# Another order of steps behind the first batch's attention in a fused attention and phase-mixing kernel

## The chip, the cores and the metric

The kernel runs on one core of a Trainium2 chip. The metric is the device time of one execution in microseconds (us); lower is better. The times below are medians over several runs. Five engines work side by side, each with its own queue in program order: TensorE (PE, matmuls and transposes into PSUM), VectorE (DVE), ScalarE (ACT), GpSimd (POOL) and SyncE (SP, which here only issues DMAs). POOL issues DMAs too.

## The reference

Two parts run one after the other, for 4 batches of 768 tokens.

```python
# 1. attention, 8 heads of 64; heads 0, 2 and 6 are causal, the others see
#    the first 4 keys and the last 64
scores = where(mask, scale * q @ k.T, -1e9)
a = exp(scores - max); a = a / sum(a)
x = a @ v                                    # heads side by side: [4, 768, 512]
# 2. phase mixing
theta = x @ w_theta                          # 512 x 512
zr, zi = x * cos(theta), x * sin(theta)
y = w_tok_r @ zr + w_tok_i @ zi              # 768 x 768, over the tokens
u = x + y
out = u + maximum(u @ w_ch, 0)               # 512 x 512
```

Inputs and the output are fp32; the kernel computes in bf16 with fp32 sums.

## The kernel before

Everything is kept in SBUF, and tokens are worked on in 6 blocks of 128. PSUM is one tile of 8 banks (`banks`), and every step that writes PSUM is told its bank or, for two banks, the first of them. Nothing is scheduled by a planner: the string `ORDER` (lines 54 to 105) is the program, a list of 812 steps. A step's name, its arguments and, at the end, its bank or its engine (D for DVE, A for ACT, P for POOL) are joined by dots. Each engine's queue holds its own steps in the order of the list, and a step waits by semaphores for what it reads, and for the readers of what it overwrites (a bank, a buffer). So a step that waits holds up all later steps of its own engine, and a bank named again makes PE wait for the reader of its last content.

The steps, with b the batch:

- `lq`, `lt`, `lw` (lines 228 to 253): POOL issues the load of one pair of heads of q or k, of a block of `w_tok`, of a weight. `lv` (234): SP issues the load of a block of v. `cv`, `bv`, `sv` copy v to bf16 (`vt`), to the block before (`vo`) and its sink rows, on the named engine.
- `tq.b.q.n.bank`, `eq`: PE turns a pair n of q or k in 12 transposes (L263), a copy brings it to `qT` or `kT` (DVE L269, ACT L267). For batch 3 the turn goes by DMA instead: `qi` joins a pair (`xi`), `qx` issues the DMA on SP, `ex` copies the result. `ko` copies keys for the streaming heads.
- `s.b.m.bank`, `e`, `m`: scores of unit m (17 units to a batch, PE L319), exp on ACT (L349), mask on DVE (L359 to L371).
- `av.b.i.bank`, `n`: a @ v of block i (PE L406), and its normalisation on DVE (L411, L413), which writes `x`.
- `xp`, `xe` turn a block of x on PE (batch 0); `xg.b.g` turns a pair of blocks by DMA from SP (the other batches).
- `wt`, `we`: a block of `w_tok` turned on PE (L442) and copied to `wtokT`.
- `th.b.g.bank` (PE L454, 8 matmuls), `tc`, `ts` (ACT L457, L460, cosine and sine into `ct` and `st`, two buffers each), `z.b.g.r/i.y` (L465): theta of two blocks, its cosine and sine, and the four products with x, called phases here, on DVE or POOL. `at` has ACT load the table of sine or exp.
- `mx.b.t.p.bank` (PE L473, 4 matmuls): output block t gets the input blocks 2p and 2p+1; three such steps fill a bank. `u` (DVE L485) adds x. `ud` turns u by DMA from SP into `uT`. `ch` (PE L489, 4 matmuls) is u @ w_ch, `o` (DVE L492) finishes it and `st` (SP) stores it; for the last block `up`, `ue`, `ca`, `oa`, `sa` do the same by PE and in halves.
- `pw.m.n.bank` (PE L512): n matmuls of ones whose result is never read.

In batch b's attention PE also does batch b-1's mixing: their steps alternate in the list. Around each theta stage (`th` of a batch) the chain is PE, ACT, DVE or POOL, then PE again. When the phases of one group are made, the third group's sine and cosine write into the buffers that the first group's phases read.

DVE's and POOL's phases are one line of the same helper:

```python
(nc.vector if eng == "D" else nc.gpsimd).tensor_tensor(z[b % 2][:, i], x[b % 2][:, i], t[:, y], ALU.mult)
```

Of the kernel before, what the change touches and what calls it, by code (L numbers as in the profile page):

```python
# [70 lines left out]
mx.0.2.1.2 s.1.4.6 m.1.15 lv.1.0 e.1.4.6 s.1.5.3 m.1.7 m.1.6 s.1.0.4 lq.2.k.2 e.1.0.4 u.0.2.2 mx.0.0.1.0 e.1.5.3 pw.0.0.6 m.1.9 mx.0.0.2.0 lq.2.q.3
wt.3.0.6 we.3.0.6.D s.1.11.2 e.1.11.2 s.1.3.4 e.1.3.4 m.1.1 lq.2.k.1 m.1.5 mx.0.0.0.0 mx.0.3.1.7 m.1.0 tq.2.k.3.2 u.0.0.0 pw.1.0.5 s.1.10.3 cv.1.1.P
bv.1.1.D m.1.12 m.1.4 m.1.3 s.1.16.0 e.1.16.0 cv.1.0.D bv.1.0.D e.1.10.3 wt.5.0.6 we.5.0.6.D lv.1.2 mx.0.3.2.7 lv.1.4 lq.2.k.0 mx.0.3.0.7 u.0.3.7
wt.5.1.0 eq.2.k.3.2.A bv.1.3.A av.1.0.5 s.1.14.2 lw.c sv.1.P n.1.0.5 e.1.14.2 we.5.1.0.D tq.2.q.3.4 eq.2.q.3.4.A tq.2.k.2.7 eq.2.k.2.7.D m.1.13 lt.4.1
# [8 lines left out]
e.2.11.6 m.2.8 e.2.5.0 mx.1.2.1.2 s.2.0.0 u.1.3.3 e.2.6.4 s.2.3.6 s.2.9.3 lq.3.q.3 qi.3.q.3.D m.2.5 qx.3.q.3 m.2.15 m.2.4 e.2.3.6 mx.1.2.2.2 m.2.6
m.2.12 mx.1.5.0.5 lq.3.k.1 st.0.0 u.1.2.2 lq.3.k.3 qi.3.k.3.D ud.1.2 mx.1.5.1.5 e.2.0.0 s.2.10.0 m.2.3 lq.3.q.2 e.2.9.3 s.2.13.6 ud.1.3 cv.2.1.P
ex.3.k.2.D e.2.13.6 m.2.0 s.2.14.3 qx.3.k.3 m.2.9 lq.3.q.1 lq.3.q.0 cv.2.3.A bv.2.3.P mx.1.5.2.5 u.1.5.5 ud.1.5 qi.3.k.1.D e.2.10.0 bv.2.1.A
mx.1.0.2.2 mx.1.0.0.2 e.2.14.3 av.2.0.0 n.2.0.0 av.2.1.5 n.2.1.5 mx.1.0.1.2 u.1.0.2 xg.2.0 m.2.13 cv.2.5.P ex.3.q.3.A bv.2.2.D av.2.2.3 n.2.2.3
cv.2.4.P bv.2.4.P st.0.2 qx.3.k.1 mx.1.1.2.0 ch.0.4.1 o.0.4.1 av.2.4.6 qi.3.q.1.A n.2.4.6 mx.1.1.0.0 ex.3.k.3.D ko.3.3.A av.2.3.1 n.2.3.1 av.2.5.6
n.2.5.6 xg.2.1 st.0.4 mx.1.1.1.0 u.1.1.0 st.0.5 s.3.8.1 e.3.8.1 xg.2.2 s.3.16.3 ch.1.3.5 th.2.0.6 ex.3.k.1.P ko.3.1.D qi.3.q.2.P ch.1.2.1 qx.3.q.1
e.3.16.3 m.3.16 tc.2.0.6 th.2.1.2 o.1.3.5 z.2.0.r.0.D z.2.0.r.1.D ts.2.0.6 z.2.0.i.0.D mx.1.4.2.4 mx.1.4.1.4 ch.1.5.0 qx.3.q.2 ex.3.q.1.D tc.2.1.2
qi.3.q.0.A th.2.2.6 mx.1.4.0.4 o.1.5.0 ts.2.1.2 ex.3.q.2.A ud.1.1 ch.1.1.3 z.2.0.i.1.P ud.1.0 o.1.2.1 z.2.1.r.1.D z.2.1.i.1.D u.1.4.4 o.1.1.3 ch.1.0.5  # L90
st.1.3 ko.3.2.D lv.3.0 z.2.1.i.0.D m.3.8 lv.3.4 tc.2.2.6 qx.3.q.0 ts.2.2.6 z.2.2.i.0.D o.1.0.5 s.3.13.0 e.3.13.0 lq.3.k.0 z.2.2.r.1.D z.2.2.r.0.D
ud.1.4 s.3.5.4 e.3.5.4 z.2.1.r.0.P s.3.3.2 qi.3.k.0.D mx.2.2.0.7 e.3.3.2 mx.2.1.0.6 mx.2.1.1.6 s.3.14.4 s.3.15.0 s.3.7.2 mx.2.2.1.7 cv.3.0.D
z.2.2.i.1.P qx.3.k.0 mx.2.1.2.6 st.1.5 e.3.7.2 ex.3.q.0.D m.3.3 mx.2.2.2.7 e.3.15.0 e.3.14.4 u.2.1.6 mx.2.5.2.2 lv.3.1 m.3.7 s.3.6.0 e.3.6.0 bv.3.0.D
sv.3.D s.3.9.5 e.3.9.5 s.3.4.3 u.2.2.7 lv.3.3 ud.2.2 e.3.4.3 lv.3.2 ex.3.k.0.P mx.2.5.0.2 mx.2.5.1.2 u.2.5.2 ud.2.5 ch.1.4.7 s.3.2.5 e.3.2.5 s.3.11.2
cv.3.4.P o.1.4.7 st.1.4 cv.3.1.D e.3.11.2 s.3.0.0 m.3.4 m.3.9 bv.3.1.D st.1.1 mx.2.3.1.4 mx.2.4.2.5 st.1.2 m.3.6 s.3.1.2 s.3.10.6 lv.3.5 e.3.0.0 m.3.2
s.3.12.0 e.3.1.2 mx.2.4.1.5 m.3.0 cv.3.3.A ud.2.1 m.3.15 mx.2.4.0.5 m.3.1 av.3.0.2 u.2.4.5 mx.2.3.2.4 bv.3.4.P m.3.13 st.1.0 m.3.5 n.3.0.2 cv.3.5.P
e.3.10.6 e.3.12.0 av.3.1.6 bv.3.3.A mx.2.3.0.4 n.3.1.6 cv.3.2.A m.3.12 ch.2.5.5 o.2.5.5 mx.2.0.2.3 av.3.2.6 xg.3.0 bv.3.2.D mx.2.0.0.3 n.3.2.6 u.2.3.4
av.3.3.1 av.3.5.6 n.3.3.1 av.3.4.4 n.3.5.6 n.3.4.4 ch.2.2.0 o.2.2.0 mx.2.0.1.3 at.1.S th.3.0.6 ts.3.0.6 u.2.0.3 z.3.0.i.0.D st.2.5 ch.2.1.1 o.2.1.1
# [503 lines left out]
```

## Time and profile before

| | |
|---|---|
| median of 3 runs | 178.44 us (178.34 to 180.28) |
| the profiled execution | 179.92 us, span 177.9 us |
| PE busy | 165.6 us, 93% of the span |
| DVE busy | 146.6 us, 82% |
| ACT busy | 117.2 us, 66% |
| POOL busy | 75.8 us, 43% |
| DMA, read and written | 180 GB/s over the span |

The span runs from the first to the last instruction of the profiled execution; its own time is 2.0 us longer. Busy time is the union of an engine's instructions. Matmuls are pipelined and their ends are modelled, so that neighbours overlap. "idle before" is the time in which an engine had nothing running ahead of an instruction, and behind the arrow stands what released it. L473 is line 473.

### The profile page before, as it was taken

To read this page: it belongs to the slowest core of one execution; us is meant where nothing else is said; L and a number is where in the kernel's file an instruction comes from. 1 tells how busy PE (TensorE), PEld (TensorE's weight loads), DVE (VectorE), ACT (ScalarE), POOL (GpSimd) and SP (SyncE) were. 2 spreads that over 40 slices of the span, in tenths; PEclk is the share of its full clock that TensorE was granted. 3 is DMA by queue.
4 is the path that set the end of the run, shared out by engine and by line. 5 is a ranking of instruction groups with operands and counts; after the bars stand their busy time and mean duration, and the time that the engine had idled before them with its cause. 6 is when DMAs were issued, how large, how long until landed. Compare 5 with 4: busy or idle time off the path is not lost.

```text
span 177.9 us, 4285 instructions
## 1 busy us (share of the span) xinstructions
PE 165.6 (93%) x1715; PEld 91.2 (51%) x1715; DVE 146.6 (82%) x286; ACT 117.2 (66%) x141; POOL 75.8 (43%) x105
## 2 busy tenths in 40 slices
...
PEclk9999999999999999999999999999999999999998
...
GB/s 172 211 172 238 201 205 145 169 220 227 206 192 177 101 151 128 218 128 149 229 237 166 192 50 281 161 197 44 179 153 292 119 133 166 89 4 59 119 263 178
DMA packets 68483, 29.90 MB, mean 168 GB/s; under 512 B 54512, under 2 KB 65520, under 8 KB 68464
## 3 DMA queue, kind: packets, MB, share of 16 engines
...
HBM read 25.69 MB, written 6.29 MB: 180 GB/s over the span
## 4 chain that ended last, share of the span: by engine, by line
PE 70%; DVE 18%; issue 7%; ACT 3%; DVEq 0%
PE banks L473 31%; PE banks L489 9%; PE banks L406 8%; PE banks L319 7%; PE banks L454 5%; PE banks L263 3%; PE banks L512 3%; DVE early L465 3%; PE banks L442 2%; DVE qT L269 2%; ACT ct L457 2%; DVE vo L269 1%; DVE zr L465 1%; DVE kT L269 1%; DVE ot L492 1%
## 5 line engine op out<-in xcount | busy, mean ns | idle before, releaser
L349 ACT ACTIVATE P<-banks 128x1024 bf16<-128x1024 f32 (+2 forms) x64 | 56.8, 946 | 13.1 <-PE banks L319 12.8
L473 PE MATMUL banks<-zr,wtokTr 128*128 128x512 bf16 x72 | 27.4, 380 | 0.0
L473 PE MATMUL banks<-early,wtokTr 128*128 128x512 bf16 x72 | 27.4, 380 | 0.0
L473 PE MATMUL banks<-early,wtokTi 128*128 128x512 bf16 x72 | 27.3, 379 | 0.0
L473 PE MATMUL banks<-zi,wtokTi 128*128 128x512 bf16 x72 | 27.3, 379 | 0.0
L489 PE MATMUL banks<-w_ch_sb,uT 128*128 128x512 bf16 x92 | 23.1, 379 | 1.2 <-DMA uT<-u 0.7
L473 PEld LDWEIGHTS <-wtokTr 128*128 128x128 bf16 x144 | 14.0, 98 | 16.1 <-issue 1.5
L319 PE MATMUL banks<-qT,kT 64*128 64x128 bf16 (+3 forms) x240 | 19.6, 247 | 2.8 <-ACT ct L457 1.6
L473 PEld LDWEIGHTS <-wtokTi 128*128 128x128 bf16 x144 | 14.1, 98 | 13.7
L269 POOL CAST vt<-st_v 128x512 bf16<-128x512 f32 x14 | 9.2, 663 | 27.3 <-DMA st_v<-in_v_dram 27.1
L371 DVE TENSOR_TENSOR P<-P,m_stream 128x1024 bf16<-128x1024 bf16 (+3 forms) x36 | 20.4, 581 | 0.4 <-ACT P L349 0.3
L460 ACT ACTIVATE st<-banks 128x1024 f32<-128x1024 f32 x12 | 12.3, 1027 | 10.9 <-PE banks L454 8.3
L406 PEld LDWEIGHTS <-P 128*128 128x128 bf16 x472 | 16.4, 97 | 3.7 <-DVE P L371 1.2
L406 PE MATMUL banks<-vt,P 128*128 128x65 bf16 x372 | 16.9, 193 | 1.0 <-DVE P L371 1.0
L492 DVE SCALAR_TENSOR_TENSOR ot<-banks,u 128x512 f32<-128x512 f32 x23 | 15.7, 691 | 2.4 <-PE banks L489 2.3
L319 PEld LDWEIGHTS <-kT 64*128 64x128 bf16 x240 | 11.0, 94 | 10.3 <-issue 7.5
L457 ACT ACTIVATE ct<-banks,half_pi 128x1024 f32<-128x1024 f32 x12 | 13.3, 1118 | 2.6 <-PE banks L454 2.3
L489 PEld LDWEIGHTS <-uT 128*128 128x128 bf16 x92 | 8.6, 98 | 11.6 <-DMA uT<-u 1.2
L269 POOL COPY vo<-vt 64x384 bf16<-64x384 bf16 (+1 forms) x9 | 9.5, 1060 | 11.0 <-DVE vt L269 6.8
L485 DVE TENSOR_TENSOR u<-early,banks 128x512 bf16<-128x512 bf16 x12 | 8.3, 689 | 6.7 <-PE banks L473 6.7
L512 PE MATMUL banks<-plain 128*128 128x384 bf16 x43 | 10.7, 378 | 2.8 <-DVE plain L191 2.2
L465 DVE TENSOR_TENSOR early<-early,ct 128x512 bf16<-128x512 bf16 x10 | 10.7, 1085 | 2.5 <-ACT ct L457 2.5
...
## 6 DMA issues: line engine op xcount, KB each, us to landing
...
```

Of the source, the lines that this page charges most:

```text
L269: (nc.vector if eng == "D" else nc.gpsimd).tensor_copy(o, i)
L319: nc.tensor.matmul(*mms[g], start=True, stop=True, skip_group_check=True)
L349: nc.scalar.activation(o, two(bank)[:, :, :o.shape[2]], AF.Exp, scale=scale)
L371: nc.vector.tensor_tensor(o, o, mk, ALU.mult)
L406: nc.tensor.matmul(o, l, r, start=(m == 0), stop=True, skip_group_check=True)
L457: nc.scalar.activation(ct[slot("ct", (b, g), TRIG_BUFS)], two(bank), AF.Sin, bias=half_pi)
L460: nc.scalar.activation(st[slot("st", (b, g), TRIG_BUFS)], two(bank), AF.Sin)
L465: (nc.vector if eng == "D" else nc.gpsimd).tensor_tensor(z[b % 2][:, i], x[b % 2][:, i], t[:, y], ALU.mult)
L473: nc.tensor.matmul(one(bank), wtokT[n][:, s, t * 128:(t + 1) * 128], z[b % 2][:, s], start=(done == 1 and s == 2 * p and n == 0), stop=(do ...
L489: nc.tensor.matmul(one(bank), uT[ti(b, t)][:, kk], w_ch_sb[:, kk], start=(kk == 0), stop=(kk == KD - 1))
L492: nc.vector.scalar_tensor_tensor(ot[oi(b, t)], one(bank), 0.0, u[ui(b, t)], ALU.max, ALU.add)
L512: nc.tensor.matmul(one(bank)[:, :384], plain[:, :128], plain, start=True, stop=True, skip_group_check=True)
```

## The change

Only `ORDER` changes, from line 62 on: behind the first batch's first two blocks of attention, up to the end. The list has the same 812 steps, but for the engine and bank at their ends and for the count of some plain matmuls, in another order.

- **Phases.** Ten go from DVE to POOL: z.0.0.i.1, z.0.1.r.0, z.0.1.i.0, z.1.2.r.0, z.2.0.r.0, z.2.0.r.1, z.2.0.i.0, z.3.0.i.0, z.3.1.i.0, z.3.2.r.1. Five go from POOL to DVE: z.1.0.r.1, z.2.0.i.1, z.2.2.i.1, z.3.0.i.1, z.3.2.i.1.
- **Copies, batch 1 and 2's keys.** To ACT: cv.1.1, cv.1.2 (from POOL), we.5.1, eq.2.k.1, ko.2.2 (from DVE). To POOL: bv.1.1 (from DVE), bv.1.2, bv.1.3 (from ACT). To DVE: cv.1.5 (from ACT), qi.3.k.2 (from POOL).
- **Copies, batch 2 and 3.** To ACT: qi.3.k.3, ex.3.k.3, ex.3.q.1, ko.3.2, bv.3.0 (from DVE), cv.2.4, bv.2.3, bv.2.4, cv.3.4, bv.3.4 (from POOL), ue.3.5 (from DVE). To POOL: cv.2.2, bv.2.2, qi.3.k.1, ko.3.1, cv.3.1, bv.3.1 (from DVE), bv.2.1, ko.3.3, qi.3.q.0, cv.3.2, bv.3.3 (from ACT). To DVE: cv.2.3, qi.3.q.1 (from ACT).
- **Steps of DVE, POOL, ACT and SP**: 216 instead of 233, 103 instead of 92, 136 instead of 130, and 91 as before.
- **Plain matmuls.** pw.9 has 2 instead of 1, and pw.0, pw.1 and pw.17 have 1 instead of 0.
- **Banks** of many steps, among them th.1.0 (2 instead of 5), th.1.1 (6 instead of 2), mx.3.3 (0 instead of 3) and up.3.5 (2 instead of 7).
- **Order.** PE: before, tq.1.q.1 stood ahead of s.1.8 and tq.1.k.0 behind it; now the other way round. th.1.0 has mx.0.4.1 ahead of it. SP: ud.1.0 stands directly ahead of xg.2.1; before, it stood seven issues behind xg.2.1. POOL: lq.2.q.0 and lq.2.q.1 stand ahead of all of batch 1's phases, bv.1.1 ahead of sv.1, and seven phases of batch 0 ahead of lt.5.1 and most of batch 2's loads. DVE: sv.3 stands behind u.2.1, u.2.2 and u.2.5; o.2.4 behind all the phases of batch 3's first two groups.

The diff at the first, second and last theta stage (the lines of one place do not match one to one):

```diff
-wt.2.0.3 xe.0.4.7.D th.0.2.5 tc.0.1.0 tq.1.q.3.4 ts.0.1.0 lt.0.1 tq.1.q.1.0 wt.2.1.2 pw.9.1.1 z.0.0.r.0.D hw.1.5 lt.0.0 tc.0.2.5 ko.1.1.D z.0.0.i.1.D
-we.2.0.3.D ts.0.2.5 z.0.2.r.0.P eq.1.q.3.4.D s.1.8.3 e.1.8.3 we.2.1.2.D eq.1.q.1.0.D tq.1.k.0.1 mx.0.2.0.2 z.0.2.i.1.P z.0.2.i.0.P wt.1.0.7
-eq.1.k.0.1.D s.1.1.0 e.1.1.0 we.1.0.7.D lt.5.0 lt.4.0 tq.1.q.2.5 eq.1.q.2.5.A lq.2.k.3 wt.3.1.6 we.3.1.6.D lt.5.1 mx.0.1.0.3 at.6.E z.0.2.r.1.D
-s.1.13.0 s.1.9.6 z.0.1.i.0.D e.1.13.0 s.1.12.4 e.1.12.4 mx.0.1.2.3 z.0.1.r.1.D e.1.9.6 z.0.1.i.1.D mx.0.2.2.2 wt.0.1.4 z.0.1.r.0.D lq.2.q.2 we.0.1.4.D
+z.0.0.i.0.P th.0.1.0 wt.2.0.3 xe.0.4.7.D tc.0.1.0 th.0.2.5 ts.0.1.0 lt.0.0 z.0.0.r.0.D z.0.0.i.1.P tc.0.2.5 hw.1.5 we.2.0.3.D tq.1.q.3.4 wt.2.1.2
+eq.1.q.3.4.D we.2.1.2.D pw.9.2.7 tq.1.k.0.1 s.1.8.3 tq.1.q.1.0 eq.1.k.0.1.D eq.1.q.1.0.D ts.0.2.5 lt.5.0 e.1.8.3 tq.1.q.2.7 z.0.2.r.0.P eq.1.q.2.7.A
+wt.1.0.6 wt.3.1.5 mx.0.2.0.2 s.1.1.0 e.1.1.0 z.0.2.i.0.P we.1.0.6.D z.0.2.i.1.P z.0.1.r.0.P we.3.1.5.D lq.2.k.3 mx.0.1.0.3 s.1.12.4 z.0.2.r.1.D
+z.0.1.r.1.D z.0.1.i.0.P lt.5.1 lq.2.q.2 z.0.1.i.1.D lq.2.q.3 e.1.12.4 s.1.9.6 s.1.13.0 e.1.13.0 e.1.9.6 mx.0.1.2.3 mx.0.2.2.2 wt.0.1.4 we.0.1.4.D
...
-n.1.5.6 wt.4.1.3 we.4.1.3.A av.1.4.1 cv.2.0.P ch.0.1.4 n.1.4.1 ko.2.2.D th.1.0.5 at.2.S lq.2.q.1 ko.2.1.D tc.1.0.5 xg.1.1 qi.3.k.2.P mx.0.4.0.0
-o.0.1.4 lq.2.q.0 ts.1.0.5 z.1.0.r.0.D z.1.0.i.1.D z.1.0.i.0.D z.1.0.r.1.P th.1.1.2 xg.1.2 th.1.2.4 tc.1.1.2 z.1.1.r.0.D mx.0.4.2.0 z.1.1.r.1.P
-ts.1.1.2 z.1.1.i.1.P ts.1.2.4 tc.1.2.4 ud.0.0 mx.0.4.1.0 u.0.4.0 ch.0.0.3 o.0.0.3 ud.0.2 tq.2.q.0.2 ud.0.3 at.5.E sv.2.P eq.2.q.0.2.D tq.2.q.1.7
+n.1.5.6 ts.1.0.2 qi.3.k.2.D o.0.1.4 mx.0.4.0.0 xg.1.2 th.1.1.6 z.1.0.r.1.D z.1.0.r.0.D z.1.0.i.1.D z.1.0.i.0.D ts.1.1.6 tc.1.1.6 z.1.1.r.0.D th.1.2.4
+mx.0.4.2.0 u.0.4.0 ts.1.2.4 tc.1.2.4 lq.2.q.1 ud.0.0 ch.0.0.6 o.0.0.6 ud.0.3 tq.2.q.0.2 eq.2.q.0.2.D z.1.1.i.0.P lv.2.3 z.1.1.r.1.P z.1.1.i.1.P
+s.2.16.0 sv.2.P s.2.8.4 tq.2.q.1.7 eq.2.q.1.7.D z.1.2.r.0.P ud.0.2 ch.0.3.3 o.0.3.3 ch.0.2.2 o.0.2.2 e.2.16.0 lv.2.2 ud.0.5 st.0.1 s.2.2.0 e.2.8.4
...
-xg.3.1 th.3.1.2 tc.3.0.6 z.3.0.r.0.D z.3.0.r.1.D xg.3.2 th.3.2.5 ts.3.1.2 tc.3.1.2 z.3.1.r.1.D z.3.1.i.0.D z.3.1.i.1.D z.3.0.i.1.P z.3.1.r.0.D ud.2.4
-ch.2.4.1 st.2.2 mx.3.4.0.0 tc.3.2.5 ud.2.3 ch.2.3.4 ts.3.2.5 mx.3.2.0.2 mx.3.3.1.3 mx.3.0.1.6 mx.3.1.1.5 o.2.3.4 z.3.2.i.1.P z.3.2.i.0.D mx.3.4.1.0
+ch.2.1.6 o.2.2.2 z.3.0.i.0.P z.3.0.i.1.D o.2.1.6 th.3.1.2 ts.3.1.2 z.3.0.r.0.D z.3.0.r.1.D ch.2.4.0 xg.3.2 th.3.2.4 z.3.1.i.0.P ud.2.0 ud.2.3 st.2.5
+st.1.4 at.1.S tc.3.1.2 z.3.1.i.1.D z.3.1.r.0.D z.3.1.r.1.D ch.2.3.3 mx.3.2.0.1 mx.3.4.0.6 o.2.4.0 o.2.3.3 st.2.3 tc.3.2.4 mx.3.3.0.0 ts.3.2.4
```

## Rows read from the trace of the kernel before

**Rows 1.** Page: engines' busy time, then the granted clock in 40 slices.

```profile
PE 165.6 (93%) x1715; PEld 91.2 (51%) x1715; DVE 146.6 (82%) x286; ACT 117.2 (66%) x141; POOL 75.8 (43%) x105
PEclk9999999999999999999999999999999999999998
```

**Rows 2.** Timeline of PE at its waits: start, length (us), what [idle before <-releaser].

```profile
37.55 0.29 PE L319 MATMUL banks<-qT,kT 64*128 64x128 bf16 x4 [0.36 <-DVE qT L269]
...
77.85 0.29 PE L319 MATMUL banks<-qT,kT 64*128 64x128 bf16 x4 [1.59 <-ACT ct L457]
78.49 0.23 PE L319 MATMUL banks<-qT,kO 64*128 64x128 bf16 x2 [0.24 <-DVE u L485]
79.09 1.24 PE L489 MATMUL banks<-w_ch_sb,uT 128*128 128x512 bf16 x5 [0.26 <-DVE ot L492]
...
116.25 1.04 PE L489 MATMUL banks<-w_ch_sb,uT 128*128 128x512 bf16 x4 [0.68 <-DMA uT<-u]
118.19 0.37 PE L319 MATMUL banks<-qT,kT 64*128 64x512 bf16 x2 [0.33 <-DVE ot L492]
...
128.66 1.02 PE L489 MATMUL banks<-w_ch_sb,uT 128*128 128x512 bf16 x4 [0.31 <-DVE u L485]
```

**Rows 3.** Busy time (x instructions) by stretch: PE, PEld, DVE, ACT, POOL.

```profile
145.00:174.00 29.00, 28.94 (x141) 13.41 (x139) 17.54 (x28) 8.95 (x10) 3.22 (x2) 1.00 0.43 121
```

**Rows 4.** Timeline of PE, a spare matmul; the same in the chain of waits.

```profile
24.51 0.33 PE L512 MATMUL banks<-plain 128*128 128x384 bf16 x1
...
24.67 0.16 PE banks L512
```

**Rows 5.** Timeline of ACT, 64 to 80 us.

```profile
68.59 1.11 ACT L457 ACTIVATE ct<-banks,half_pi 128x1024 f32<-128x1024 f32 x1 [1.03 <-PE banks L454]
75.77 1.02 ACT L460 ACTIVATE st<-banks 128x1024 f32<-128x1024 f32 x1 [2.56 <-DVE early L465]
```

**Rows 6.** Timeline of DVE, 70 to 80 us.

```profile
69.74 2.75 DVE L465 TENSOR_TENSOR early<-early,ct 128x512 bf16<-128x512 bf16 x1 [1.68 <-ACT ct L457]
72.41 3.24 DVE L465 TENSOR_TENSOR early<-early,st 128x512 bf16<-128x512 bf16 x2
75.58 2.27 DVE L465 TENSOR_TENSOR early<-early,ct 128x512 bf16<-128x512 bf16 x1
```

**Rows 7.** Timeline of POOL, 69.5 to 79 us.

```profile
70.02 0.72 POOL L231 DMA_DIRECT2D qb<-in_q_dram  x1
70.76 1.17 POOL L465 TENSOR_TENSOR early<-early,ct 128x512 bf16<-128x512 bf16 x1
75.05 2.24 POOL L269 COPY vo<-vt 4x1920 bf16<-4x1920 bf16 x1
```

**Rows 8.** Groups by shape: count | busy us, mean ns | idle before.

```profile
L465 DVE TENSOR_TENSOR zr<-x,ct 128x512 bf16<-128x512 bf16 x10 | 6.8, 696 | 2.9 <-ACT ct L457 2.9
L465 POOL TENSOR_TENSOR zr<-x,ct 128x512 bf16<-128x512 bf16 x2 | 2.3, 1172 | 0.6 <-ACT ct L457 0.6
```

**Rows 9.** Timeline of POOL, 33 to 48 us.

```profile
33.70 1.68 POOL L465 TENSOR_TENSOR zi<-x,st 128x512 bf16<-128x512 bf16 x1 [1.36 <-ACT st L460]
45.77 0.72 POOL L231 DMA_DIRECT2D kb<-in_k_dram  x1
```

**Rows 10.** Timeline of DVE, 39.5 to 47 us.

```profile
41.61 0.68 DVE L465 TENSOR_TENSOR zr<-x,ct 128x512 bf16<-128x512 bf16 x1
```

**Rows 11.** DMA into kb (38 to 60 us), then uT (100 to 120 us).

```profile
DMA to landing us min/median/max: 3.8/8.3/10.2
DMA to landing us min/median/max: 2.4/2.5/4.6
```

**Rows 12.** DMA issues of one kind: count, median us to landing.

```profile
early<-early SPq DMA_TRANSPOSE x6, 3.2
```

**Rows 13.** Timelines of POOL, then DVE, 54 to 66 us.

```profile
55.29 1.87 POOL L269 COPY vo<-vt 4x1920 bf16<-4x1920 bf16 x1 [6.76 <-DVE vt L269]
...
60.53 0.69 DVE L413 TENSOR_TENSOR early<-banks,rr 128x512 bf16<-128x512 f32 x1
```

More of the change, by code (lines that the diff above doesn't have):

```diff
@@ L61 @@
 s.0.5.3 e.0.5.3 s.0.14.6 e.0.14.6 pw.35.6.0 s.0.13.2 s.0.16.0 e.0.16.0 m.0.4 m.0.8 av.0.0.4 k.half av.0.1.6 m.0.7 e.0.13.2 s.0.9.0 lq.1.k.2 m.0.5 lw.t
-n.0.0.4 n.0.1.6 lt.2.0 pw.24.4.2 tq.1.k.3.5 e.0.9.0 tq.1.q.0.3 xp.0.0.2 pw.3.1.4 m.0.13 lq.1.q.1 bv.0.2.A m.0.9 eq.1.q.0.3.A cv.0.3.P xp.0.1.0
-tq.1.k.1.1 bv.0.1.P pw.4.0.4 xe.0.1.0.D xe.0.0.2.A cv.0.4.A eq.1.k.1.1.A av.0.3.6 av.0.2.3 tq.1.k.2.2 wt.1.1.0 eq.1.k.2.2.A lq.1.q.3 lt.2.1 bv.0.3.D
+n.0.0.4 n.0.1.6 lt.2.0 pw.24.4.2 tq.1.k.3.5 e.0.9.0 tq.1.q.0.3 xp.0.0.2 pw.3.1.4 m.0.13 lq.1.q.1 bv.0.2.A m.0.9 eq.1.q.0.3.A cv.0.3.P xp.0.1.7
@@ L64 @@
+tq.1.k.1.1 bv.0.1.P pw.4.0.4 xe.0.1.7.D xe.0.0.2.A cv.0.4.A eq.1.k.1.1.A av.0.3.6 av.0.2.3 tq.1.k.2.2 wt.1.1.0 eq.1.k.2.2.A lq.1.q.3 lt.2.1 bv.0.3.D
 m.0.16 n.0.3.6 eq.1.k.3.5.A n.0.2.3 at.0.S we.1.1.0.D bv.0.4.P av.0.4.6 n.0.4.6 xp.0.3.1 cv.0.5.P xe.0.3.1.A av.0.5.3 xp.0.2.2 xe.0.2.2.D ko.1.2.P
-lq.1.k.0 th.0.0.5 tc.0.0.5 lq.1.q.2 lt.1.0 ko.1.3.P lt.3.1 n.0.5.3 xp.0.5.4 xe.0.5.4.D lt.3.0 xp.0.4.7 ts.0.0.5 z.0.0.r.1.D z.0.0.i.0.P th.0.1.0
-wt.2.0.3 xe.0.4.7.D th.0.2.5 tc.0.1.0 tq.1.q.3.4 ts.0.1.0 lt.0.1 tq.1.q.1.0 wt.2.1.2 pw.9.1.1 z.0.0.r.0.D hw.1.5 lt.0.0 tc.0.2.5 ko.1.1.D z.0.0.i.1.D
@@ L71 @@
[L71 to L74, printed above, removed]
@@ L83 @@
[L83 to L86, printed above, removed]
@@ L87 @@
[L87 to L98, printed above, removed]
@@ L103 @@
-st.3.0 mx.3.5.0.3 u.3.5.3 ch.3.1.4 o.3.1.4 st.3.1 ch.3.3.6 o.3.3.6 st.3.3 up.3.5.7 ch.3.2.0 ue.3.5.7.D o.3.2.0 at.4.E ch.3.4.3 st.3.2 o.3.4.3 st.3.4
-ca.3.5.1.4 oa.3.5.1.4 ca.3.5.0.2 oa.3.5.0.2 sa.3.5.1 at.3.S sa.3.5.0
+lq.1.k.0 th.0.0.5 tc.0.0.5 lq.1.q.2 lt.1.0 ko.1.3.P lt.3.1 ko.1.1.D n.0.5.3 xp.0.5.4 xe.0.5.4.D lt.3.0 xp.0.4.7 ts.0.0.5 z.0.0.r.1.D lt.0.1
+z.0.0.i.0.P th.0.1.0 wt.2.0.3 xe.0.4.7.D tc.0.1.0 th.0.2.5 ts.0.1.0 lt.0.0 z.0.0.r.0.D z.0.0.i.1.P tc.0.2.5 hw.1.5 we.2.0.3.D tq.1.q.3.4 wt.2.1.2
```

38 lines of the change are left out of this document (30 added, 8 removed).

## Prediction

> **What bounds the kernel.** I read the page first. [...] Next I read PE's timeline and step starts for waits behind 23 us, where the change begins. There are four places [rows 2]: (a) 0.36 at 37.55, for a copy of batch 1's query; (b) 1.59 + 0.24 + 0.26 = 2.09 at 77.85 to 79.09, behind batch 1's phases; (c) 0.68 at 116.25, for a turned u, and 0.33 at 118.19, for a bank; (d) 0.31 at 128.66, for a bank. That is 3.77. In a stream without waits a matmul starts before the modelled end of the one ahead: the spare at 24.51 is 0.33 long and takes 0.16 of the chain [rows 4]. Each of the seven waits hides up to 0.16 so, and what they cost lies between 3.8 and 4.9; I take 4.7, since all follow a full stream. The last 29 us are busy for 28.94 [rows 3]: nothing can be gained there.
>
> The profiled execution took 179.9 us, 2.0 around its span of 177.9. The runs' median is 178.44, so I subtract from that.
>
> **Place (b) first, the largest.** The chain runs through three engines. Batch 1's first theta ends as ACT's cosine starts, 68.59 [rows 5]. DVE then needs 2.75 + 3.24 + 2.27 for four phases, until 77.85 [rows 6]; one alone takes 0.696 [rows 8]. In that time POOL issues a load, runs phases and the copy of the sink values [rows 7], and DVE's phases end about 0.56 after POOL's work: 70.76 + 1.17 + 0.56 = 72.49, and 75.05 + 2.24 + 0.56 = 77.85. So the two engines take turns. The sine of group 2 reuses a buffer that these phases read and waits 2.56, to 75.77 [rows 5]; the cosine behind it frees the bank at 77.80, and u and finish sit behind the phases in DVE's queue. That is all of (b).
>
> After the change POOL has its two loads behind it before the cosine, the phase z.1.0.r.1 and the join qi.3.k.2 are DVE's, and POOL's first phase needs the sine of group 1. Counted from the first theta's end E: cosine E + 1.1, four DVE phases of 0.7 to E + 3.9, POOL's first phase from about E + 3.6. The second theta ends at E + 2.6 and ACT's last four (two of 1.02, two of 1.11, overlapped by 0.1) free the bank at E + 6.6, against 9.2 before. PE wants it at E + 6.7. So (b) goes whole; next late is the load of batch 2's query 1, with a margin of about 1.5.
>
> **What that stage now waits for.** The sink copy (1.87 at 55.29 [rows 13]) stands behind bv.1.1 on POOL, which waits for cv.1.1, now ACT's, until about 57.2. So it runs from 57.8 across two DVE masks and delays norm 1 by 0.6 to 1.3. The old norm 1 ended at 61.22 [rows 13] and its turn takes 3.2 to land [rows 12]: 64.4, while theta started near 66.7. The cover of 2.2 holds it; without it 0 to 1.3 would be on the path. ACT gets five steps more between 56 and 65 and loses three: one spare (pw.17) waits about 0.1 for its copy. On SP, ud.0.2 moves behind one load of v; its landing (2.4 to 4.6 for such turns [rows 11]) meets its matmuls within 0.5. I take 0.3 for these, ends 0 and 1.4.
>
> **Place (a).** The sink keys' copy moves ahead and z.0.0.i.1 goes to POOL, so DVE copies the query 0.3 sooner, and a key's transposes fill PE. (a) goes.
>
> **The phases of batch 0.** POOL now starts at 33.70 [rows 9] on seven phases and three loads before the last is done: 1.68 + 6 x 1.17 + 3 x 0.7 = 10.8, so 44.5, and up to 1.2 more if DVE takes turns. mx.0.1.1 wants it at 45.2. DVE's two copies, two masks and u.0.1 stand behind the last of its own phases, and s.1.5.3 takes that u's bank. The wait is 0 to 1.2; I take 0.4. The loads behind these phases move too: lq.2.k.1 goes out near 49.5 instead of 45.77 [rows 9]. Its landing takes 8.3 at the median and 10.2 at worst [rows 11], and its transposes come at 58.8: 0 at the median, 0.9 at worst; I take 0.
>
> **Spares.** Four more plain matmuls: 4 x 0.16 = 0.64 [rows 4]. One stood in wait (a) anyway.
>
> **Place (c).** ud.1.0 is issued ahead of xg.2.1 instead of after ud.1.1, several us earlier; its turn took 4.6, the longest [rows 11]. The wait goes, the next late is the bank of s.3.3, behind a finish that has two phases and a long copy fewer ahead of it on DVE. ACT loses two joins and gains two long copies, about even. I leave 0.2 of this place.
>
> **Place (d).** bv.3.0 goes to ACT, sv.3 behind the u's: it goes. But POOL's copy ex.3.k.0 may lie across u.2.1, whose bank s.3.9 needs: 0 to 1.4, I take 0.2.
>
> **Batch 3.** o.2.4 now stands behind seven of DVE's phases, and mx.3.3.0 takes its bank 0. From third-batch theta's start S: PE gets there at S + 9.5; DVE at S + 8.7 to 10.8, as POOL's two phases do or do not lie across. 0 to 1.4, I take 0.7. The tail (ue.3.5 on ACT, other banks) has 1.7 of matmuls over it: 0.
>
> **The sum.** -4.7 + 0.3 + 0.4 + 0.64 + 0.2 + 0.2 + 0.7 = -2.3: **176.1 us**. With every added wait at its worst (1.4 + 2.1 + 0.64 + 0.2 + 1.4 + 1.4 = 7.1, less 4.7) it is 180.8; with the spares alone, and 4.9 gone, 174.2.
>
> [...] The change gives POOL ten of DVE's phases and takes five back, five more of 1.17 [rows 8]. At 70.02 to 72.49 a DVE phase waited through a load issue and a POOL phase [rows 6, 7], yet at 41.61 one took 0.68 beside a load issue [rows 10]. [...]
>
> **Rivals.** *The waits move (0.31)*: the additions cost 3 to 4.5 instead of 2.4, as ACT's chain of exps behind (b) keeps its time, and with 3.7 it is 177.4. For it: DVE is busy 82% of the span; against it: (b) and (c) have causes that the new queues take away. [...]
>
> **The chances.** The forecast has 0.55, in a likely band of 174.5 to 176.6; these two have the rest. About 1% (1.8 us) is what a measurement of this kernel can tell. So faster 0.55, same 0.31, slower 0.14. The range of 174.2 to 179.8 leaves out the slow rival and little more.
>
> **What would show it.** Right: PE without idle time between the two transposes of q and ch.0.3 in batch 1, DVE's four phases near 0.7 each, no wait on a turned u in batch 2. Wrong: DVE's phases of batch 0 or 1 above 1 us, PE waiting for u.0.1's or o.2.4's bank for over 1.5, a transpose waiting for batch 2's keys.

## The result, and the profile after

The changed kernel takes 180.54 us at the median (20 runs) against 179.03 for the kernel before beside it (20 runs): ratio 1.0106, 95% interval 1.0073 to 1.0138, some 1.9 us slower. In a later comparison the ratio was 1.0040 (0.9984 to 1.0095), 0.7 us slower. An unchanged copy of the kernel before came out at 1.0031 (0.9990 to 1.0071); so one comparison was off by 0.3%, and the two of the changed kernel differ by 0.7%. The forecast was 2.3 us faster, which neither interval holds. (All ratios leave out runs over 1.5% above the fastest run of the same kernel.)

The profiled execution of after took 180.19 us, span 178.2; that of before 179.92, span 177.9. So the two traces differ by 0.3, while the medians differ by 1.5. That gap is the clue: the traced execution of before was longer than its usual run.

The page of after: busy time of the engines, against [rows 1].

```profile
PE 164.4 (92%) x1698; PEld 91.0 (51%) x1719; DVE 139.5 (78%) x266; ACT 119.0 (67%) x146; POOL 84.5 (47%) x118
PEclk9999999999999999999999999999999999999999
```

The granted clock averaged 1.00 of full speed from 0 to 174 us in both traces, so that the two differ in what PE does and waits for.

PE's timeline of after at its waits (start, length, what, in brackets the idle time before it and its releaser), against [rows 2]:

```profile
43.85 0.38 PE L473 MATMUL banks<-zr,wtokTr 128*128 128x512 bf16 x1 [0.45 <-DVE zr L465]
...
78.42 0.81 PE L489 MATMUL banks<-w_ch_sb,uT 128*128 128x512 bf16 x3 [0.16 <-issue]
...
103.65 0.23 PE L319 MATMUL banks<-qT,kO 64*128 64x128 bf16 x2 [0.73 <-POOL kO L269]
...
104.53 0.82 PE L454 MATMUL banks<-w_theta_sb,xT 128*128 128x512 bf16 x3 [0.32 <-DMA xT<-x]
...
118.32 0.27 PE L319 MATMUL banks<-qT,kT 64*128 64x256 bf16 x1 [1.52 <-ACT ct L457]
118.83 0.39 PE L319 MATMUL banks<-qT,kT 64*128 64x128 bf16 x3 [0.24 <-DVE ot L492]
...
129.02 0.81 PE L489 MATMUL banks<-w_ch_sb,uT 128*128 128x512 bf16 x3
```

Of the seven waits of [rows 2] six are gone, and the bank of s.3.3 is still waited for (0.24); at 78.42 (ch.0.3) and 129.02 (ch.1.4) nothing is waited for. (0.16 ahead of three matmuls instead of four is a record that is missing.) In their place stand 0.45 at mx.0.1.2, in batch 0's phases; 0.73 + 0.32 at s.3.16 and th.2.0; and 1.52 at s.3.5 ahead of the 0.24, in place (c).

DVE's timeline of after, in the theta stages of batch 0, 1 and 2, against [rows 6]:

```profile
40.71 4.66 DVE L465 TENSOR_TENSOR zr<-x,ct 128x512 bf16<-128x512 bf16 x2
...
71.97 1.29 DVE L465 TENSOR_TENSOR early<-early,ct 128x512 bf16<-128x512 bf16 x2 [2.31 <-ACT ct L457]
73.18 1.28 DVE L465 TENSOR_TENSOR early<-early,st 128x512 bf16<-128x512 bf16 x2
...
113.34 3.76 DVE L465 TENSOR_TENSOR zi<-x,st 128x512 bf16<-128x512 bf16 x1
117.03 0.55 DVE L371 TENSOR_TENSOR P<-P,m_stream 128x768 bf16<-128x768 bf16 x1
117.50 0.67 DVE L485 TENSOR_TENSOR u<-early,banks 128x512 bf16<-128x512 bf16 x1
118.10 0.68 DVE L492 SCALAR_TENSOR_TENSOR ot<-banks,u 128x512 f32<-128x512 f32 x1
```

POOL's, in the first and the last of these stages, against [rows 7]:

```profile
41.41 1.16 POOL L465 TENSOR_TENSOR zr<-x,ct 128x512 bf16<-128x512 bf16 x1
42.51 0.77 POOL L231 DMA_DIRECT2D kb<-in_k_dram  x1
43.30 1.52 POOL L465 TENSOR_TENSOR zi<-x,st 128x512 bf16<-128x512 bf16 x1
...
112.80 1.07 POOL L269 COPY kO<-kT 64x320 bf16<-64x320 bf16 x2
113.82 0.82 POOL L269 COPY xi<-qb 128x768 bf16<-128x768 bf16 x1
114.59 0.76 POOL L231 DMA_DIRECT2D kb<-in_k_dram  x1
115.37 1.18 POOL L465 TENSOR_TENSOR zr<-x,ct 128x512 bf16<-128x512 bf16 x1
```

Batch 1's four phases on DVE take 2.5 together, as forecast (8.3 in [rows 6]). But at 113.34 a phase that takes 0.7 alone lasts 3.76: POOL runs four instructions (copy, join, load's issue, phase) without a gap, and the phase ends 0.55 behind the last of them (115.37 + 1.18 + 0.55 = 117.10). Behind it in DVE's queue stand u.1.4, which frees the bank of s.3.5, and o.1.1, which frees that of s.3.3. They end at 118.17 and 118.78; PE goes on at 118.32 and 118.83. The trace names ACT's cosine as the releaser, which ended at 118.28: two candidates 0.1 apart, for experiments.

### The profile page after: what moved, and what is told of

Same layout as the page of the kernel before. It is cut to its first block, busy times and chain, and to the rows that moved or that the text cites. A ratio compares the mean times of both kernels' runs of the same rounds, so it can differ in the third digit from the quotient of the medians.

```text
span 178.2 us, 4276 instructions
## 1 busy us (share of the span) xinstructions
PE 164.4 (92%) x1698; PEld 91.0 (51%) x1719; DVE 139.5 (78%) x266; ACT 119.0 (67%) x146; POOL 84.5 (47%) x118
## 4 chain that ended last, share of the span: by engine, by line
PE 68%; DVE 15%; DMA 7%; issue 4%; POOL 2%; DVEq 0%; SPq 0%
PE banks L473 31%; PE banks L454 10%; PE banks L489 9%; PE banks L319 6%; PE banks L406 6%; DMA kb<-in_k_dram 3%; PE banks L263 3%; DMA xT<-x 3%; DVE zr L465 2%; PE banks L442 2%; DVE qT L269 2%; DVE P L371 2%; DVE kT L269 2%; DVE ot L492 2%; DMA out_dram<-ot 1%
## 5 line engine op out<-in xcount | busy, mean ns | idle before, releaser
L473 PE MATMUL banks<-zr,wtokTr 128*128 128x512 bf16 x64 | 24.3, 380 | 0.4 <-DVE zr L465 0.4
L473 PE MATMUL banks<-early,wtokTr 128*128 128x512 bf16 x65 | 24.7, 380 | 0.0
L371 DVE TENSOR_TENSOR P<-P,m_stream 128x1024 bf16<-128x1024 bf16 (+3 forms) x36 | 23.8, 674 | 0.6 <-ACT P L349 0.5
L489 PE MATMUL banks<-w_ch_sb,uT 128*128 128x512 bf16 x87 | 22.0, 379 | 0.4 <-issue 0.2
L269 POOL COPY vo<-vt 64x384 bf16<-64x384 bf16 (+1 forms) x13 | 11.0, 848 | 16.2 <-ACT vt L267 15.8
L319 PEld LDWEIGHTS <-kT 64*128 64x128 bf16 x240 | 10.8, 94 | 10.2 <-issue 7.8
L512 PE MATMUL banks<-plain 128*128 128x384 bf16 x47 | 11.5, 368 | 2.6 <-DVE plain L191 2.2
L267 ACT COPY uT<-banks 128x512 bf16<-128x512 bf16 x1 | 0.6, 586 | 18.0 <-PE banks L432 18.0
```

What stands on the lines that cost most here:

```text
L269: (nc.vector if eng == "D" else nc.gpsimd).tensor_copy(o, i)
L319: nc.tensor.matmul(*mms[g], start=True, stop=True, skip_group_check=True)
L371: nc.vector.tensor_tensor(o, o, mk, ALU.mult)
L473: nc.tensor.matmul(one(bank), wtokT[n][:, s, t * 128:(t + 1) * 128], z[b % 2][:, s], start=(done == 1 and s == 2 * p and n == 0), stop=(do ...
L489: nc.tensor.matmul(one(bank), uT[ti(b, t)][:, kk], w_ch_sb[:, kk], start=(kk == 0), stop=(kk == KD - 1))
L512: nc.tensor.matmul(one(bank)[:, :384], plain[:, :128], plain, start=True, stop=True, skip_group_check=True)
```

## The experiments

My theories: **T1**, the second half of the list loses what the first gains, by DVE being kept out at batch 2's theta; rivals **R1**, ACT's copy ex.3.q.1 ahead of that theta's last cosine is the cause, and **R2**, the gain of 2.1 at place (b) was never there.

**Halves.** Before's and after's lists were joined at s.2.7 (about 80 us).

```diff
 z.1.2.i.1.D qx.3.k.2 e.2.1.6 s.2.7.4
-mx.1.3.0.3 ch.0.5.0 e.2.7.4 at.5.E z.1.2.i.0.D
+at.5.E bv.2.0.D m.2.16 m.2.1 e.2.7.4 mx.1.3.0.3
...
```

> After's list up to the scores s.2.7 (about 78 us: place (a), batch 0's phases, the theta stage of batch 1), then before's order for all the rest. Theory (the second half loses): the first half is worth the 0.67 by which ch.0.3 is earlier in the trace of after plus the 0.34 by which that trace was late from its start, so 1.0 us under before. Rival (the gain at (b) is eaten in the first half, by the phases that POOL takes in batch 0 and the spares, or by ACT's chain of exps): no gain, 0 to 1 us over before.

Measured: 1.0019 (0.9993 to 1.0044), no gain. R2's number, though PE has no wait left at (b). From after, at 1.0106, it differs behind the join alone: the loss lies there.

```diff
 lv.2.3 qx.3.k.2 e.2.1.6 s.2.7.4
-m.2.1 e.2.7.4 mx.1.3.0.3 ch.0.5.0
+z.1.1.i.0.P lv.2.2 lq.3.q.3 z.1.2.i.1.D mx.1.3.0.3 ch.0.5.0
...
```

> The other half: before's list up to s.2.7, then after's order. Theory: all of the loss is here, the 1.9 of after against before plus the 1.0 that its first half gains, so 2 to 3 us over before. Rival: within 0.5 of before, since (d) and the turned u gain what the rest loses. PE would be seen waiting before s.3.16 and s.3.5.

Measured: 1.0130 (1.0079 to 1.0181), 2.3 us over. The size proves little: the ratio rests on two of six runs, and in the trace PE also waits 2.10 at s.2.12 for o.0.5, which the join put late and which neither before nor after has. But the waits of 1.51 and 0.24 at s.3.5 and s.3.3 are there again (none at s.3.16). So with e1 the loss is in the second half, as T1 has it, and the gain of the first isn't there.

**Is the wait at (b) in every run?**

> Before once more, unchanged, for a second trace of it. If the 2.09 of place (b) is in every run, PE waits 1.5 or more at s.2.8 again and DVE's four phases take over 7 together. If it was an accident of the one run (which took 179.9, while the median was 178.4), the phases take 3 to 5 together and PE waits under 0.5 there. Time 179.0 either way.

The second trace of before (time 178.17, span 176.1): DVE's four phases in place (b):

```profile
69.66 0.69 DVE L465 TENSOR_TENSOR early<-early,ct 128x512 bf16<-128x512 bf16 x1 [0.63 <-ACT ct L457]
70.57 1.95 DVE L465 TENSOR_TENSOR early<-early,st 128x512 bf16<-128x512 bf16 x2 [0.22 <-ACT st L460]
72.44 1.64 DVE L465 TENSOR_TENSOR early<-early,ct 128x512 bf16<-128x512 bf16 x1
```

PE in places (b), (c) and (d):

```profile
71.70 1.47 PE L454 MATMUL banks<-w_theta_sb,early 128*128 128x512 bf16 x6 [0.63 <-DMA early<-early]
77.41 1.90 PE L489 MATMUL banks<-w_ch_sb,uT 128*128 128x512 bf16 x8
...
114.83 1.04 PE L489 MATMUL banks<-w_ch_sb,uT 128*128 128x512 bf16 x4 [1.00 <-DMA uT<-u]
126.94 1.02 PE L489 MATMUL banks<-w_ch_sb,uT 128*128 128x512 bf16 x4 [0.31 <-DVE u L485]
```

POOL ahead of place (b), and then what the trace says of the load lv.2.0 alone:

```profile
65.91 0.62 POOL L269 CAST vt<-st_v 128x512 bf16<-128x512 f32 x1 [6.00 <-PE banks L406]
```

```profile
DMA to landing us min/median/max: 3.3/3.3/3.3
```

The same two views of the first trace of before:

```profile
67.97 0.62 POOL L269 CAST vt<-st_v 128x512 bf16<-128x512 f32 x1 [7.99 <-DMA st_v<-in_v_dram]
```

```profile
DMA to landing us min/median/max: 5.2/5.2/5.2
```

From 16 to 64 us the steps of PE, DVE, ACT and POOL start within 0.1 of each other in the two executions of before. Then in the first the load landed 1.9 later, POOL's copy of it began at 67.97 instead of 65.91, and the load issue, join, load issue and phase queued behind it met DVE's phases instead of being over. In the second trace ch.0.3 starts at 77.41 without a wait, against 79.09, and PE stays 1.7 ahead to the last matmul: this stretch makes all but 0.1 of the difference between the two. The traces of e2 (above) and e12 (below), with before's order there, have no such wait either. The 2.09 of place (b) is in one trace of four, an accident of that run; why the load was late stays open.

```diff
-xg.1.0 m.1.16 lv.2.0 eq.2.k.1.0.D
+xg.1.0 m.1.16 eq.2.k.1.0.D
...
-tc.1.0.5 xg.1.1 qi.3.k.2.P
+tc.1.0.5 xg.1.1 lv.2.0 cv.2.0.P lq.2.q.1 qi.3.k.2.P
```

> Before with two issues on SP changing places, the load lv.2.0 behind the turn xg.1.1 instead of ahead of it, and nothing else on any queue; so POOL's copy cv.2.0 waits for the load until 68 to 69 instead of 65.9. If a late copy there sends POOL's load, join, load and phase against DVE's phases, the four phases of DVE take 7 or more together, PE waits 1.5 or more at s.2.8, and the run is 1.2 to 2.2 over before. If the wait in the first trace had another cause, within 0.4 of before.

Measured: 1.0372 (1.0317 to 1.0428), 6.6 us over. POOL's copy:

```profile
75.89 0.92 POOL L269 CAST vt<-st_v 128x512 bf16<-128x512 f32 x1 [14.54 <-DMA st_v<-in_v_dram]
```

DVE's second and third phase (the third alone took 7.38):

```profile
76.56 8.10 DVE L465 TENSOR_TENSOR early<-early,st 128x512 bf16<-128x512 bf16 x2 [0.22 <-ACT st L460]
```

PE at s.2.8:

```profile
86.85 0.40 PE L319 MATMUL banks<-qT,kT 64*128 64x128 bf16 x4 [2.63 <-ACT ct L457]
```

The path is shown: load, copy, POOL's run, DVE, the sine that reuses a buffer, PE. The size was 3 to 5 times what I expected. In this trace the turn ahead of the load, a wait of 2.70 for a late key load at 62.66 (not the edit's doing) and the load itself put the copy off to 75.89 instead of 68 to 69, and batch 2's last q loads stand behind that copy on POOL (another 2.00 at a transpose). The granted clock averaged 0.89 of full speed between 60 and 76 us, 0.79 between 76 and 92 and 1.00 between 92 and 130, and the scores behind the wait at 86.85 took 0.34 for two matmuls where e5 has 0.22; the clock's mean was under 0.99 in all seven runs, so not all of the 6.6 is waiting.

```diff
 av.1.3.3 cv.1.4.P cv.1.5.A n.1.3.3
-we.4.0.2.A bv.1.4.A mx.0.5.0.5 u.0.5.5
+ko.2.2.A we.4.0.2.A xg.1.1 mx.0.5.0.5
...
```

> Before with only the stretch of place (b) in after's order (from the third norm of batch 1 to s.2.7), nothing else. If place (b) costs 2.1 in every run of before, this is 1.5 to 2.1 us under before. If that wait was an accident of the profiled run, it is within 0.6 of before.

Measured: 1.0039 (1.0004 to 1.0074): no gain, 0.7 us over. PE waits 1.01 for the turn xg.1.2 at th.1.2, where the second trace of before has 0.63, and nothing at ch.0.3 in either. R2 holds.

**What holds s.3.5?**

```diff
-ch.1.0.5 ex.3.q.1.A m.3.16 u.1.4.4 o.1.1.2 z.2.1.i.1.D o.1.0.5 ts.2.2.6 tc.2.2.6 s.3.5.4
+ch.1.0.5 m.3.16 u.1.4.4 o.1.1.2 z.2.1.i.1.D o.1.0.5 ts.2.2.6 tc.2.2.6 ex.3.q.1.A s.3.5.4
```

> After, with the copy ex.3.q.1 on ACT moved from ahead of batch 2's last sine and cosine to behind them. If ACT is what holds s.3.5 at 118.3 (the trace names its cosine), s.3.5 then waits for this copy alone, until 117.8, and the run is 0.5 to 1.0 us under after. If DVE holds it (u.1.4 ended at 118.17, behind a phase of 3.76), nothing changes: within 0.3 of after.

Measured: 1.0059 (1.0036 to 1.0082), 0.8 us under after by the first comparison of that and 0.3 over it by the second, so the time doesn't decide. The trace does: the cosine now ends at 115.53, and PE's wait is the same, with DVE as its releaser (PE's timeline of e3). R1 falls.

```profile
117.52 0.27 PE L319 MATMUL banks<-qT,kT 64*128 64x256 bf16 x1 [1.52 <-DVE u L485]
118.03 0.39 PE L319 MATMUL banks<-qT,kT 64*128 64x128 bf16 x3 [0.24 <-DVE ot L492]
```

```diff
-z.2.1.i.0.D ch.1.1.2 ch.1.0.5 ex.3.q.1.A m.3.16 u.1.4.4 o.1.1.2 z.2.1.i.1.D
+ch.1.1.2 ch.1.0.5 ex.3.q.1.A m.3.16 u.1.4.4 o.1.1.2 z.2.1.i.0.D z.2.1.i.1.D
```

> After, with DVE's phase z.2.1.i.0 moved behind u.1.4 and o.1.1 (it took 3.76 us beside four POOL instructions in a row, and these two stood behind it). [...] If ACT's copy is the cause: within 0.3 of after.

Measured: 1.0013 (0.9986 to 1.0041), 0.8 us under e3 in the same comparison. But the wait only fell to 0.90: the mask m.3.16, next in the queue, was kept out instead (0.55 in after). DVE's timeline of e4:

```profile
113.17 3.62 DVE L371 TENSOR_TENSOR P<-P,m_stream 128x768 bf16<-128x768 bf16 x1
116.72 0.68 DVE L485 TENSOR_TENSOR u<-early,banks 128x512 bf16<-128x512 bf16 x1
```

So I moved the mask too, on a kernel with the old count of spares (plain matmuls). First the spares alone, against e4:

```diff
-we.2.1.2.D pw.9.2.7 tq.1.k.0.1
+we.2.1.2.D pw.9.1.7 tq.1.k.0.1
...
-we.5.0.6.D pw.1.1.5 pw.0.1.6 m.1.3
+we.5.0.6.D pw.1.0.5 pw.0.0.6 m.1.3
...
-mx.0.5.1.5 pw.17.1.0 av.1.2.6
+mx.0.5.1.5 pw.17.0.0 av.1.2.6
```

> After with u.1.4 and o.1.1 ahead of the phase z.2.1.i.0, as in the run before that had it (0.2 over before), and the spare matmuls as before (four fewer). If each spare costs its 0.16 on PE's chain, 0.5 to 0.7 under before; if they stand in waits, as before, 0 to 0.3 over it.

Measured: 0.9997 (0.9953 to 1.0040), 0.3 us under e4 of another comparison: less than 0.64, within the noise. The traces settle the price: from mx.0.2.2 to av.2.0 PE takes 50.50 in after, e3, e4, e6 and e10, which have three spares more in that stretch, and 50.01 in e8, e9, e11, e13 and e14, which don't: 0.16 each. (e16 has another wait there.)

Then the mask:

```diff
-ex.3.q.1.A m.3.16 u.1.4.4 o.1.1.2 z.2.1.i.0.D z.2.1.i.1.D
+ex.3.q.1.A u.1.4.4 o.1.1.2 z.2.1.i.0.D m.3.16 z.2.1.i.1.D
```

> After with the old count of spares and, on DVE, both the phase z.2.1.i.0 and the mask m.3.16 behind u.1.4 and o.1.1. With the phase alone moved, the mask took 3.62 in its place and s.3.5 still waited 0.90. If any DVE instruction that works on SBUF alone is kept out by POOL's run of four, while u.1.4 and o.1.1, which read PSUM, are not, u.1.4 ends by 116.0 and the waits at s.3.5 and s.3.3 (0.90 + 0.24) go; 0.5 to 0.8 under the run with the phase alone moved, so 0.5 under before. If an instruction that reads PSUM is kept out too, u.1.4 takes over 1.5 and nothing is gained.

Measured: 0.9950 (0.9912 to 0.9988). DVE's timeline in place (c):

```profile
114.76 0.69 DVE L485 TENSOR_TENSOR u<-early,banks 128x512 bf16<-128x512 bf16 x1 [1.66 <-PE banks L473]
115.68 0.69 DVE L492 SCALAR_TENSOR_TENSOR ot<-banks,u 128x512 f32<-128x512 f32 x1 [0.23 <-PE banks L489]
116.28 0.68 DVE L465 TENSOR_TENSOR zi<-x,st 128x512 bf16<-128x512 bf16 x1
```

POOL's phase beside it:

```profile
115.04 1.18 POOL L465 TENSOR_TENSOR zr<-x,ct 128x512 bf16<-128x512 bf16 x1
```

PE at mx.2.1.0:

```profile
118.01 0.38 PE L473 MATMUL banks<-zr,wtokTr 128*128 128x512 bf16 x1 [0.97 <-ACT ct L457]
```

u.1.4 and o.1.1, which read a bank and one tile of SBUF, took 0.69 each beside POOL's work. The waits at s.3.5 and s.3.3 are gone. Now the cosine is late, 0.97.

The next run goes back to after and moves one phase:

```diff
-s.3.13.0 lq.3.k.0 z.2.1.r.0.P z.2.2.i.1.D
+s.3.13.0 lq.3.k.0 z.2.1.r.0.D z.2.2.i.1.D
```

> After with one phase, z.2.1.r.0, given back to DVE, so that POOL's run at batch 2's theta is a copy, a join and a load's issue instead of these and a phase. If a load's issue keeps DVE out as a POOL instruction does, DVE's z.2.1.i.0 ends about 0.56 after that issue (near 115.9); if not, 0.56 after the join (near 115.2). Either way s.3.5 waits under 0.6 instead of 1.5, and the run is 0.8 to 1.2 under after. If POOL's run isn't what holds the phase, it takes over 3 again.

Measured: 1.0001 (0.9956 to 1.0045). DVE's phase:

```profile
112.94 1.83 DVE L465 TENSOR_TENSOR zi<-x,st 128x512 bf16<-128x512 bf16 x1
```

POOL's last two instructions there:

```profile
113.41 0.82 POOL L269 COPY xi<-qb 128x768 bf16<-128x768 bf16 x1
114.18 0.76 POOL L231 DMA_DIRECT2D kb<-in_k_dram  x1
```

The phase ended 0.54 behind the join, beside the load's issue, which did not keep it out. PE's wait at s.3.5 went. That POOL's run holds DVE is shown by taking its last phase away: 1.83 instead of 3.76. The issue at 42.51 in after, with a phase behind it, does seem to have kept DVE out: its phase ended at 43.80, 0.52 behind the end of that issue.

The next edit is to e9:

```diff
-z.0.2.i.1.P z.0.1.r.0.P we.3.1.5.D lq.2.k.3 mx.0.1.0.3 s.1.12.4 z.0.2.r.1.D z.0.1.r.1.D z.0.1.i.0.P
+z.0.2.i.1.P z.0.1.r.0.D we.3.1.5.D lq.2.k.3 mx.0.1.0.3 s.1.12.4 z.0.2.r.1.D z.0.1.r.1.D z.0.1.i.0.D
```

> The kernel e9 with two phases of batch 0, z.0.1.r.0 and z.0.1.i.0, back on DVE. In after DVE's z.0.2.r.1 took 3.09 there behind three POOL instructions and mx.0.1.2 lasted 1.64 instead of 1.03. If that is the cost of batch 0's phases, mx.0.1.2 lasts 1.03 again and the run is 0.5 to 0.6 under e9. If the two phases on DVE only put mx.0.1.1 or u.0.1 later, no gain.

Measured: 0.9890 (0.9843 to 0.9937), the lowest ratio, below both kernels. mx.0.1.2 runs without its gap, but a copy of w_tok behind z.0.1.r.0 (1.75) is now late by 0.37, so only 0.25 is gained by mx.0.2.2. Of the 2.0 between the spans of the two traces most is the wait at s.3.16, which this trace doesn't have (1.16 in e9's) and which comes and goes between executions. The intervals of e9 and e11 overlap, so only the 0.25 can be put down to the two phases.

**The turns by DMA.**

```diff
-e.3.8.1 xg.2.2 s.3.16.3
+e.3.8.1 xg.2.2 ud.1.0 s.3.16.3
...
-z.2.0.i.1.P ud.1.0 o.1.2.1
+z.2.0.i.1.P o.1.2.1
```

> Before with one issue moved: the turn ud.1.0 on SP goes directly behind xg.2.2, ahead of qx.3.q.1, qx.3.q.2 and ud.1.1. In the second trace of before PE waits 1.00 for this turn at ch.1.0. If the wait goes and nothing takes its place, 0.7 to 1.0 under before. If the two turns of batch 3 that are now 1.25 later hold ACT's sines or DVE's phases instead, 0.

Measured: 1.0026 (0.9987 to 1.0066), no gain, by neither of the causes I had named. PE now waits at ch.1.1, for ud.1.1 (PE's timeline; then that turn's time to landing).

```profile
114.46 1.90 PE L489 MATMUL banks<-w_ch_sb,uT 128*128 128x512 bf16 x8 [1.83 <-DMA uT<-u]
```

```profile
DMA to landing us min/median/max: 4.5/4.5/4.5
```

ud.1.0 landed in 2.8 this time. The slow turn is the one that SP issues within 0.4 of POOL's issue of the load lq.3.k.0, whichever it is: ud.1.0 in both traces of before (4.6 and 4.5), ud.1.1 here. In after, where that load goes out 4.5 behind ud.1.1, ud.1.1 landed in 2.6; but ud.1.0, 6.6 behind POOL's last issue of a load, took 4.1 there. So the load as the cause is neither shown nor tried alone.

```diff
-cv.2.2.P lq.3.k.1 cv.2.5.P
+cv.2.2.P lq.3.k.1 lq.3.q.1 lq.3.q.2 cv.2.5.P
...
-cv.2.1.P lq.3.q.1 u.1.5.5
+cv.2.1.P u.1.5.5
...
-ex.3.q.3.A lq.3.q.2 mx.1.1.2.0
+ex.3.q.3.A mx.1.1.2.0
```

> The kernel e11 with the loads lq.3.q.1 and lq.3.q.2 issued directly behind lq.3.k.1 (near 85) instead of near 92 and 95, where the turns qx.3.k.3 to xg.2.0 are issued. If turns issued while such a load is in flight land late, those turns land within 3 of their issue instead of 4 to 6.7, and the wait at s.3.16 (0.7 to 1.2 in half of the traces) can't come: 0 to 0.5 under e11. If only the number of bytes in that stretch counts, the lateness moves to ud.0.4 and the loads of v ahead of av.2.0, and PE waits there or for ch.0.4: 0 to 1 over e11.

Measured: 0.9983 (0.9933 to 1.0033), not under e11. qx.3.k.3 landed in 4.3 instead of 6.1, and no wait came at s.3.16, but PE reached it 0.9 later than in e11, counted from av.2.0: the lateness moved ahead of it, as the second expectation has it. PE waits at av.2.1 for POOL's copy of v:

```profile
97.09 0.28 PE L406 MATMUL banks<-vt,P 128*128 128x65 bf16 x4 [0.78 <-POOL vt L269]
```

```diff
-ch.1.0.5 ex.3.q.1.A u.1.4.4
+ch.1.0.5 u.1.4.4
...
-ts.2.2.6 tc.2.2.6 s.3.5.4 s.3.3.2 s.3.13.0 lq.3.k.0 z.2.1.r.0.P z.2.2.i.1.D z.2.2.r.0.D z.2.2.r.1.D mx.2.1.0.6
+ts.2.2.6 tc.2.2.6 ex.3.q.1.A mx.2.1.0.6 s.3.5.4 s.3.3.2 s.3.13.0 lq.3.k.0 z.2.1.r.0.P z.2.2.i.1.D z.2.2.r.0.D z.2.2.r.1.D
```

> The kernel e11 with ACT's copy ex.3.q.1 behind batch 2's last sine and cosine, and mx.2.1.0 on PE ahead of s.3.5, s.3.3 and s.3.13, which wait for that copy. With after's DVE order moving the copy changed nothing; now DVE is out of the way and PE waits 0.68 at mx.2.1.0 for the cosine. If ACT is what is late next, that wait goes: 0.5 to 0.7 under e11. If the copy is now late for s.3.5 by as much, 0.

> The edits of e13 and of e14 together on e11. If both work, the fastest: 0.5 to 1.2 under e11, some 2.5 to 3 under before.

Measured: e14 0.9936 (0.9897 to 0.9976), e16 0.9973 (0.9935 to 1.0011). In e14's trace the wait of 0.68 is gone and its span is 174.4 against 174.9 in e11; the time is not measurably better. e16 keeps e13's loss (1.53 at av.2.1; s.3.16 is 1.7 later than in e11, counted from av.2.0).

> After once more, for its time beside the others on one chip and a second trace. [...]

Measured: 1.0040, 0.7 us over before; the waits at s.3.5 and s.3.3 are there again, 1.50 and 0.24, as T1 has it, and there is none at s.3.16. But PE also waits 1.49 at s.3.9, for u.2.1 behind two DVE steps that lie across POOL's copies ex.3.k.0 and cv.3.1; e2's trace has the same:

```profile
128.19 0.21 PE L319 MATMUL banks<-qT,kO 64*128 64x128 bf16 x1 [1.49 <-DVE u L485]
```

In both, the granted clock was not at full speed throughout: its mean was 0.991 in e6's trace and 0.969 in e2's, where single scores of 64x128 take 0.31 from 122.64 on, between the two waits, for 0.21 to 0.22 in e3. In the traces of after, e3 and e4 the mean was 1.000, and there is no wait at s.3.9.

## Why the prediction was wrong

- **The size of place (b), "2.09", is the term that failed.** The mechanism was read rightly (POOL's work in DVE's way, the sine's buffer, the bank), and after's trace has no such wait. But of four traces with before's order there, one has it. I had a hint of it: the profiled execution took 179.9, 1.5 over the median, and I took its waits off the median. POOL's row at 67.97 names a load as what began it; I didn't follow the chain that far. In the second trace the waits are (a) 0.36, the turn at th.1.2 0.63, (c) 1.00 and, for the bank of s.3.3, 0.22, (d) 0.31: 2.52, where I had 3.77, and 4.7 with the overlaps.

```profile
116.47 0.37 PE L319 MATMUL banks<-qT,kT 64*128 64x512 bf16 x2 [0.22 <-DVE ot L492]
```

- **Place (c), "I leave 0.2", was mis-sized the other way.** The wait on a turned u went, but 1.52 + 0.24 came, and it was in all four traces with DVE's and POOL's order of after there (after, e2, e3, e6). e4, e9 and e10 show the cause. I looked at ACT's joins and at SP; POOL's run of copy, join, load and phase across DVE's z.2.1.i.0 I had priced only for batch 0 and batch 1.
- **That ud.1.0 earlier frees (c)** holds in after's order, where no trace waits for a turned u in batch 2's theta stage; alone it hands the wait to ud.1.1 (e12).
- **The slow rival (0.14)** came nearest in time: 180.54 lies above the range that leaves it out. POOL's work did hold DVE, but at other places than I had looked at. In batch 0 DVE lost 3.3 in two phases (4.66 for 1.4) and PE 0.45. That I gave 0.4 is luck: I had it at mx.0.1.1 or s.1.5.3, and it came at mx.0.1.2, for DVE's z.0.2.r.1. In batch 1 z.1.1.r.0 lost next to nothing (0.75).
- **What held:** (a), ACT's chain at (b) (the bank free at E + 6.5, forecast E + 6.6), POOL's 10.8 us in batch 0, the loads behind them, the sink copy's cover, 0.16 for each spare. (d) held in after, e3 and e4; the 1.49 at s.3.9 of e2 and e6 is its worst case, "0 to 1.4", and a little more. Batch 3's 0.7 was not spent, but only just: o.2.4 ended at 153.78 and mx.3.3.0 started at 153.83. (It stands behind six of DVE's phases, where I counted seven.)
- **Not foreseen:** 0.73 + 0.32 at s.3.16, where ex.3.k.3's turn took 6.7 to land. It is in some traces of after's order (after, e8, e9, e10) and not in others (e2, e3, e4, e6, e11, e14).

Put together for after's trace: 2.81 of listed waits, 0.45, and 0.64 for spares, against 2.52 in the second trace of before: 1.4 more, with five waits on each side, so that the overlaps cancel. From tq.1.k.3 to the last half block it is 149.88 against 148.21, 1.67 more; 0.3 of it I can't place. The first trace of before has 149.86 there: beside that one the changed order looks even. Against the forecast of -2.3, the waits to be taken away were put 2.2 too high and place (c) 1.6 too low, 1.05 at s.3.16 and th.2.0 was not foreseen, and 1.2 was given to waits that did not come.
